# Clustered attention, a Fourier step and a feed-forward net in one Trainium2 kernel: rows 129 to 256 of the transform folded some ticks ahead of the sequence's end, sign images of two weight pieces at a time, and power-of-two scales worked out by way of PSUM

## The chip, the core and the metric

The kernel runs on one core of a Trainium2 chip. A core has five engines that run in parallel, each through its own list of instructions in order: PE (TensorE, matrix products), DVE (VectorE), ACT (ScalarE), POOL (GpSimd) and SP (which here only issues DMA transfers). Engines wait for one another through semaphores. Data lie in SBUF (128 partitions) and in PSUM, into which PE writes its products and which DVE and ACT read and write as well. The metric is the device time of one execution in microseconds (us).

## The reference

Inputs are q, k and v (4 sequences x 8 heads x 768 rows x 64), 16 centroids of 64 numbers for each head, and two weight matrices (512 x 2048 and 2048 x 512), all float32.

```
q_n, k_n, c_n = q/|q|, k/|k|, centroids/|centroids|
mask   = argmax_c(q_n . c_n)[:, None] == argmax_c(k_n . c_n)[None, :]
attn   = softmax(where(mask, q @ k.T / 8, -1e9))      # rows over 768 keys
x      = concat over heads of attn @ v                # 4 x 768 x 512
mixed  = real(fft(fft(x, axis=1), axis=2))            # over 768 rows, then 512 columns
u      = x + mixed
un     = (u - mean(u)) / sqrt(var(u) + 1e-6)          # per row
out    = u + relu(un @ w_ch1) @ w_ch2
```

A row attends only to keys of its own cluster. The real part of the two transforms needs, of a transform over 512 columns, cosine and sine products; since cosine is even and sine odd, column 512-j can be added to (or subtracted from) column j first, which halves the product. The same holds over the 768 rows. The kernel calls both steps folding.

## The kernel before, in words

**Number format.** A float32 operand of a product is written as two float16 halves (high and low), and the product is made of three float16 products. Making the halves is called halving: ACT writes the high half, DVE the low one (`halve`, L641 and L642). Each tensor is first scaled by a power of two that is found from its largest magnitude: `top_power` (L55 to L61) takes the exponent's bits with a shift (L58), an addition with a maximum (L59) and a minimum with a multiplication (L60), and ends with a reciprocal (L61); the first three work in integers on a few numbers per partition.

**Attention.** Two heads of one sequence make a pair, 16 pairs in all (pair 0 to 15, four per sequence). Each pair has six steps of 128 rows; a step is called a tick here, and tick n is step (n - 5) mod 6 of pair (n - 5) // 6, so that pair 4, the first of the second sequence, begins at tick 29. In a tick, `scores` makes the products of 128 rows with all 768 keys for both heads into two PSUM tiles (L320), adds the mask by a product of cluster codes (L325, whose operand `oht` is the transposed "one-hot" code), then DVE scales them and finds the row's largest (L339), ACT takes the exponential (L343 for pairs 0 to 3, L345 later) and writes its high half (L353), POOL the low half (L354), and SP issues a transposing DMA of each half (L356). One tick later `attend` multiplies them with v (L374 to L376), and DVE divides by the row sums into the tile X (L386 to L390). X holds [128, 6, 512]: the 768 x 512 rows of one sequence; there are two X tiles, used in turn. For pairs 0 to 3 the second X tile serves as the exponential's buffer; from pair 4 on, L339 writes its output to a bf16 tile `ju` that nobody reads (only the row's largest is used), and L345 reads PSUM.

**One-hot codes.** For the next pair, products with the centroids stand in a PSUM slot; DVE subtracts the largest into the tile `ac` (L277, L279), POOL adds a term for ties (L281), DVE finds the largest again (L285) and writes the codes (L289, L293), POOL two small parts of them (L298, L300), and SP transposes them into `oht` (L303). `ac` has one buffer.

**Weights.** In ticks 0 to 28 the weights are loaded in 32 pieces of 128 x 512 and changed to halves: a DMA into one of eight raw buffers, the largest magnitude (L491), then for the first matrix one scale per row block (L496 or L504, then `top_power`, 128x1 or 128x4), two ACT instructions that take two sign images of the top 16 bits (`signs`, L519 and L520, 128x512 each, into one of two buffers `PN`), a product that joins them to the piece (PE L528, DVE L532), and halving (L538, L541, L542, L544). A PSUM pool `psf` of three 128x512 slots serves this, the scales, the Fourier step and the feed-forward net.

**Fourier and feed-forward.** Sequence b's attention ends two ticks after its last step, at tick 31, 55, 79 and 103. There `fold` runs: it subtracts X's row blocks 3 to 5 from blocks 0 to 2 (L660, 128x1536), folds the columns (L661, 128x765, on DVE for the subtraction and on POOL for the sum), halves 256 columns (L641, L642, 128x768) and transposes both halves in one DMA (L667); then the same for the sum. Both use one buffer `XF`. The transform's products (L713, L728), the row transform, the norm, `up` (L858) and `down` (L888) of sequence b are spread over the ticks of sequence b + 1's attention; after tick 103 there is no attention left and they run alone.

**Order.** PE's order is written by hand: a planner gives each call a tick and a place in the tick (for instance `at(t, 0, self.fft.fold, b)`), and fills the ticks with the Fourier and feed-forward products up to a due time. The other engines' orders are decided by a scheduler from the same calls, so that code placed elsewhere moves instructions of other work as well.

## Time and profile before

| what | value |
|---|---|
| runs shown, us | 1053.73, 1049.66, 1053.15 (median 1053.15) |
| profiled execution: own time, us | 1049.91 |
| its span (first to last instruction), us | 1048.1 |
| PE busy | 910.8 us, 87% |
| DVE busy | 627.4 us, 60% |
| ACT busy | 625.3 us, 60% |
| POOL busy | 586.9 us, 56% |
| mean share of the 16 DMA engines, 45 to 205 us | 0.96 |

Times in rows are microseconds from the start of the span, unless marked ns. A group's row reads: line, engine, operation, output <- inputs with shapes, count | busy time, mean ns of one | idle time of that engine just before them and what ended it. A row of waits reads: engine, what it was about to do <- engine and instruction (or transfer) that it waited for: total us, times, longest. A row of the timeline reads: start, duration, engine, instruction, and in brackets the idle time before it. A row of windows gives a stretch's length, then busy us (and count) of PE, PE's weight loads, DVE, ACT and POOL, the granted PE clock, and the share of DMA. Ticks are not marked in the profile; they are counted from the groups of L320. In this execution tick 25 begins at 177.4, 29 at 206.1, 31 at 219.6, 33 at 246.4, 50 at 393.0, 74 at 614.1; the last sequence's fold (tick 103) begins at 882.5. Attention's last tick begins at 854.9.

### The profile page before, as it was taken

Reading aid. Unit: us, or ns where it says so; the run is one execution under the profiler, and the core shown is the slowest. Engines: PE = TensorE matmul, PEld = TensorE weight load, DVE = VectorE, ACT = ScalarE, POOL = GpSimd, SP = SyncE. Lnnn points to the kernel's source line nnn. Section 1 sums busy time; section 2 is a strip of 40 time slices with the busy share of each in tenths; the row PEclk is TensorE's granted clock in tenths of the full one; section 3 lists DMA queues with packets and bytes.
Section 4 is the critical chain, followed back from the end, with each engine's and each line's share of the span. In section 5 each row is a group of like instructions: output and inputs, shape, how many; then the busy total and the mean of one; then the engine's idle time right before and its main releaser. Section 6 shows DMA issues by size and latency. Waiting matters only on the chain.

```text
span 1048.1 us, 23542 instructions
## 1 busy us (share of the span) xinstructions
PE 910.8 (87%) x9350; PEld 591.7 (56%) x9362; DVE 627.4 (60%) x1297; ACT 625.3 (60%) x980; POOL 586.9 (56%) x693
## 2 busy tenths in 40 slices
PE   3665565749899999998899999997999999999998
PEld 2333333425575756655666757555757667576674
DVE  8789899767757555668656555667555333631110
ACT  4798889755766665645666746556756543351230
POOL 2364565753975756655856646647847645271230
PEclk9987878769899999999899999998999999999999
DMA  7799998979887776568877767588757562321000
GB/s 272 179 225 245 196 239 166 171 156 153 177 123 153 128 154 121 121 137 161 153 137 142 140 128 132 110 141 170 124 102 133 96 110 43 81 52 31 11 11 21
DMA packets 396239, 140.01 MB, mean 134 GB/s; under 512 B 381784, under 2 KB 381792, under 8 KB 396128
## 3 DMA queue, kind: packets, MB, share of 16 engines
q1 hardware_dynamic: 396128, 138.50, 65.9%
q8 instruction: 73, 1.20, 0.5%
q14 instruction: 38, 0.31, 0.1%
HBM read 42.52 MB, written 6.29 MB: 47 GB/s over the span
## 4 chain that ended last, share of the span: by engine, by line
PE 39%; DVE 6%; DMA 3%; ACT 3%; POOL 2%; issue 2%; SPq 0%; ACTq 0%; DVEq 0%; POOLq 0%
PE ps_f L888 16%; PE ps_f L858 13%; PE ps_big L320 3%; DMA pt<-ph 3%; PE ps_f L713 2%; DVE ju L339 1%; ACT p L345 1%; PE ps_o L374 1%; POOL ph L354 1%; PE ps_o L375 1%; PE ps_o L376 1%; PE ps_big L325 1%; ACT ph L353 1%; DMA scr<-in_k_dram 0%; DVE arena L660 0%
## 5 line engine op out<-in xcount | busy, mean ns | idle before, releaser
L354 POOL TENSOR_TENSOR ph<-p,ph 128x768 f16<-128x768 f32 x144 | 242.9, 1688 | 184.6 <-ACT ph L353 150.1
L858 PE MATMUL ps_f<-arena,w1h 128*128 128x256 f16 x1536 | 271.4, 277 | 19.1 <-ACT arena L866 9.0
L888 PE MATMUL ps_f<-w2h,arena 128*128 128x512 f16 x768 | 238.9, 379 | 0.0
L345 ACT ACTIVATE p<-ps_big,rmx,sce 128x768 f32<-128x768 f32 x144 | 142.1, 988 | 132.9 <-DVE ju L339 127.5
L858 PE MATMUL ps_f<-arena,w1l 128*128 128x256 f16 x768 | 212.4, 277 | 0.0
L339 DVE TENSOR_SCALAR_CACHE_REDUCE ju<-ps_big,sce 128x768 bf16<-128x768 f32 x144 | 146.1, 1014 | 68.2 <-PE ps_big L325 58.2
L888 PEld LDWEIGHTS <-arena 128*128 128x128 f16 x1152 | 108.7, 98 | 126.6 <-issue 5.2
L858 PEld LDWEIGHTS <-w1h 128*128 128x128 f16 x1536 | 152.1, 99 | 36.0 <-issue 14.3
L867 POOL TENSOR_TENSOR arena<-arena 128x256 f16<-128x256 f32 x192 | 128.1, 677 | 77.3 <-ACT arena L866 73.6
L320 PE MATMUL ps_big<-hlk,hlq 64*128 64x384 f16 x1152 | 128.9, 348 | 39.0 <-ACT p L345 23.4
L374 PE MATMUL ps_o<-v,pt 128*128 128x66 f16 x1152 | 124.8, 198 | 43.0 <-DVE X L390 27.5
L888 PE MATMUL ps_f<-w2l,arena 128*128 128x512 f16 x384 | 145.5, 379 | 0.0
L374 PEld LDWEIGHTS <-pt 128*128 128x128 f16 x1152 | 110.2, 100 | 57.7 <-issue 37.1
L353 ACT CAST ph<-p 128x768 f16<-128x768 f32 x144 | 119.6, 832 | 15.0 <-DMA pt<-ph 12.8
L375 PE MATMUL ps_o<-v,pt 128*128 128x64 f16 x1152 | 124.8, 199 | 0.0
L376 PE MATMUL ps_o<-v,pt 128*128 128x66 f16 x1152 | 124.5, 198 | 0.0
L866 ACT ACTIVATE arena<-ps_f,wrel 128x256 f16<-128x256 f32 x192 | 90.1, 472 | 54.8 <-DVE arena L863 54.7
L863 DVE TENSOR_SCALAR arena<-ps_f,wrel 128x256 f32<-128x256 f32 x96 | 46.3, 482 | 124.9 <-PE ps_f L858 66.4
L320 PEld LDWEIGHTS <-hlq 64*128 64x128 f16 x1152 | 55.5, 99 | 101.5 <-issue 72.7
L375 PEld LDWEIGHTS <-pt 128*128 128x128 f16 x1152 | 110.7, 101 | 2.8
L376 PEld LDWEIGHTS <-pt 128*128 128x128 f16 x1152 | 111.1, 103 | 0.0
L858 PEld LDWEIGHTS <-w1l 128*128 128x128 f16 x768 | 76.1, 99 | 20.2 <-issue 10.7
(178 smaller groups left out, 1330.4 us busy)
## 6 DMA issues: line engine op xcount, KB each, us to landing
arena<-in_moe_w_ch_dram SPq DMA_DIRECT2D x32, 512.0 KB, 6.8
scr<-in_q_dram SPq DMA_DIRECT2D x16, 384.0 KB, 2.9
scr<-in_k_dram SPq DMA_DIRECT2D x16, 384.0 KB, 4.5
vst<-in_v_dram SPq DMA_DIRECT2D x16, 384.0 KB, 3.5
out_dram<-arena SPq DMA_DIRECT2D x24, 256.0 KB, 2.3
pt<-ph SPq DMA_TRANSPOSE x168, 3.9
arena<-in_cs_dram SPq DMA_DIRECT2D x12, 192.0 KB, 3.5
arena<-in_ss_dram SPq DMA_DIRECT2D x12, 192.0 KB, 3.5
```

Of the source, the lines that this page charges most:

```text
L320: nc.tensor.matmul(out=ps[j][:, hf, 0:SH], lhsT=hq[rows[j], a, sl], rhs=hk[rows[j], c, hs], start=(i == 0), stop=False)
L339: self.mark = nc.vector.tensor_scalar(out=ju, in0=ps[j][:, :, 0:SH], scalar1=ne, scalar2=None, op0=ALU.mult, op1=ALU.min, accum_out=m)
L345: nc.scalar.activation(x, ps[j][:, :, 0:SH], AF.Exp, bias=m, scale=e)
L353: nc.scalar.copy(out=ph[:, 0], in_=p32)
L354: nc.gpsimd.tensor_tensor(out=ph[:, 1], in0=p32, in1=ph[:, 0], op=ALU.subtract)
L374: nc.tensor.matmul(out=o[:, at:at + W], lhsT=hi, rhs=v16[:, kt, 0:W], start=(kt == 0), stop=False)
L375: nc.tensor.matmul(out=o[:, at:at + D], lhsT=hi, rhs=v16[:, kt, 66:130], start=False, stop=False)
L376: nc.tensor.matmul(out=o[:, at:at + W], lhsT=lo, rhs=v16[:, kt, 0:W], start=False, stop=(kt == ST - 1))
L858: nc.tensor.matmul(out=ps.rearrange("p (t x) -> p t x", x=P), lhsT=a[:, dc, fs], rhs=c[:, :, dc], start=(i == 0), stop=(i == 11))
L866: nc.scalar.activation(hh[:, f], ps, AF.Relu, scale=rel[:, f:f + 1])
L867: nc.gpsimd.tensor_tensor(out=hl[:, f], in0=r, in1=hh[:, f], op=ALU.subtract)
L888: nc.tensor.matmul(out=ps, lhsT=a[:, f, ts], rhs=c[:, f], start=(i == 0), stop=(i == 47))
```

## The change

Four things are changed.

**Scales by way of PSUM.** `top_power` gets a second operand `t` for its intermediate results. For 128x1 it is the PSUM column into which the largest is now reduced; for 128x4 it is four columns of a fresh `psf` slot (four times in the run). L58, L59 and L60 then read or write PSUM; only L60's result and the reciprocal stay in SBUF.

**Signs of two pieces.** `signs` runs for every second piece and takes two pieces in one instruction, 128x1024, into buffers `PN2`.

**L339 in place.** For pairs 4 to 15, L339 writes its scaled scores over the scores in PSUM, in float32, and the exponential reads them with scale -1; `ju` is gone, and the arena of SBUF that the weights and the Fourier step share grows by 3072 B per partition.

**The fold in two halves.** Column j is folded with column 512-j, so columns 128 to 255 need X's column blocks 1 and 2 only (128 columns each, written by a sequence's second and third pair), and columns 0 to 127 blocks 0 and 3. `early` folds, halves and transposes the first kind, the difference six ticks and the sum four ticks ahead of the sequence's end (ticks t-6 and t-4 for t = 31, 55, 79, 103), in a tile taken from `ac`, pinned behind the tick's last L339. `fold` at tick t does the rest: DVE adds 128x768, then 128x381, ACT and DVE halve 128x384 instead of 128x768, and each transposing DMA moves 6 blocks instead of 12 (four DMAs of 6 per sequence for two of 12). All folding is on DVE now; POOL's L661 goes, five small POOL copies come. The two folds of `fold` have a buffer each. The columns 0, 128 and 256 that stand at the seams change places, and the constants with them (`dft_constants`, `c128`, `first`); `even` and `odd` take columns 128 to 255 first.

Knobs that come with it (`KEEP0`, `WAIT`, `N1`) have the values that leave the order of the calls as it was. PE's list is the same as before but for the operands' names. The lists of the others change: DVE has 36 rows more, ACT 24 fewer, POOL 16 more, SP 8 more.

```diff
-def top_power(nc, tops, s, inv):
-    t = tops.bitcast(I32)
-    nc.vector.tensor_scalar(out=t, in0=t, scalar1=20, scalar2=None, op0=ALU.logical_shift_right)
+def top_power(nc, tops, t, s, inv):
+    t = t.bitcast(I32)
+    nc.vector.tensor_scalar(out=t, in0=tops.bitcast(I32), scalar1=20, scalar2=None, op0=ALU.logical_shift_right)
     nc.vector.tensor_scalar(out=t, in0=t, scalar1=-910.0, scalar2=1.0, op0=ALU.add, op1=ALU.max)
...
-            ju = x if early else sb.tile([P, 2, SH], BF16, name="ju", tag="ju")
+            ju = x if early else ps[j][:, :, 0:SH]
             self.mark = nc.vector.tensor_scalar(out=ju, in0=ps[j][:, :, 0:SH], scalar1=ne, ..., accum_out=m)
-                nc.scalar.activation(x, ps[j][:, :, 0:SH], AF.Exp, bias=m, scale=e)
+            nc.scalar.activation(x, ju, AF.Exp, bias=m, scale=-1.0)
...
     def scales(self, g, mx):
         s = self.sb.tile([P, 4], F32, name="wsc", tag="wsc", bufs=2)
-        top_power(self.nc, mx, s[:, 0:n], ...)
+        t = self.psf()[:, 0:n] if n > 1 else mx
+        top_power(self.nc, mx, t, s[:, 0:n], ...)
...
     def signs(self, k):
+        if self.JOINT:
+            if k % 2 == 0:
+                pn = at(self.PN2[k // 2 % 2], [P, 2, 2, DM], BF16)
+                raw = at(self.RAW[k % len(self.RAW)], [P, 2, 4 * DM + 16], U16)
+                top = raw[:, :, 4:4 + 4 * DM].rearrange("p a (n f) -> p a n f", f=4)[:, :, :, 0]
+                nc.scalar.activation(pn[:, 0].bitcast(I16), top.bitcast(I16), AF.Relu, ...)
+                nc.scalar.activation(pn[:, 1].bitcast(I16), top, AF.Relu, ...)
+            return
...
+    def prepared(self, b, buf, blocks, i, op):
+        nc.vector.tensor_tensor(out=buf.rearrange("p (z t x) -> p t z x", z=2, t=3), in0=x[0], in1=x[1], op=op)
+        f = buf.rearrange("p (z t x) -> p z t x", z=2, t=3)
+        first, second = f[:, 0, :, 0:1], f[:, 1, :, 0:1]
+        if blocks[0]:
+            nc.gpsimd.tensor_copy(out=self.c128[:, i], in_=first)
+            if i == 0:
+                nc.gpsimd.tensor_copy(out=first, in_=second)
+        else:
+            if i == 0:
+                nc.gpsimd.tensor_copy(out=self.first, in_=first)
+            nc.vector.tensor_tensor(out=first, in0=self.c128[:, i], in1=second, op=op)
+        nc.vector.tensor_tensor(out=f[:, 0, :, 1:P], in0=f[:, 0, :, 1:P], in1=f[:, 1, :, P - 1:0:-1], op=op)
+        h = buf[:, SH:2 * SH].bitcast(F16).rearrange("p (a t x) -> p a t x", a=2, t=3)
+        self.halve(f[:, 0], h[:, 0], h[:, 1], self.scale[b][0])
+        t = self.arena.at(self.XT[i][blocks[0]], [P, 6, P], F16)
+        nc.sync.dma_start(out=t, in_=h.rearrange("p a t x -> p (a t x)"), transpose=True)
+
+    def early(self, b, k):
+        i, op = self.FOLDS[k]
+        buf = self.pool.tile([P, 2, ST * 4, NC_], F32, name="ac", tag="ac").rearrange("p a g c -> p (a g c)")
+        self.parts[b][i, 1] = self.prepared(b, buf, (1, 2), i, op)
+
     def fold(self, b):
         for i, op in self.FOLDS:
-            f = at(self.XF, [P, 3, DM], F32)
-            self.engine(self.FE[i]).tensor_tensor(out=f, in0=X[:, 0:3], in1=X[:, 3:6], op=op)
-            self.engine(self.FE[2 + i]).tensor_tensor(out=f[:, :, 1:M], in0=f[:, :, 1:M], in1=f[:, :, DM - 1:M:-1], op=op)
-            h = at(self.XH, [P, 2, 3, M], F16)
-            self.halve(f[:, :, 0:M], h[:, 0], h[:, 1], s)
-            nc.sync.dma_start(out=t, in_=h.rearrange("p a t x -> p (a t x)"), transpose=True)
+            buf = at(self.XF + 3072 * i, [P, 2 * SH], F32)
+            self.parts[b][i, 0] = self.prepared(b, buf, (0, 3), i, op)
...
+    E, KEEP0 = (-6, -4), 21.0
...
             at(t, -1, self.drain, self.KEEP0)
+            for k in range(2):
+                at(t + self.E[k], 4.6, pin, self.fft.early, b, k)
             at(t, 0, self.fft.fold, b)
```

Three places in DVE's list of instructions show how the change moves work. Rows read: line of that version, operation, output<-inputs, shape, and x2 for two in a row. L491, L532, L544, L660, L642, L390, L388 and L386 of before are L489, L540, L552, L666, L655, L387, L385 and L383 of the change.

DVE in the weights' stage, at the second of the four 128x4 scales and the finish of attention's rows beside it (116 us in the profile; X_63 is the first X tile, X_64 the second, winv_86 the table of inverse scales). Before:

```order
L386 TENSOR_SCALAR rs<-ps_o,scp 128x6
L289 TENSOR_TENSOR oh<-ac,mx 128x12x16
L293 TENSOR_TENSOR oh<-ac,mx 128x6x16 x2
L532 SCALAR_TENSOR_TENSOR ps_f<-arena,ps_f 128x512 x2
L388 RECIPROCAL rs<-rs 128x6
L339 TENSOR_SCALAR X_64,rmx<-ps_big,sce 128x768 x2
L390 TENSOR_TENSOR X_63<-ps_o,rs 128x3x128
L491 TENSOR_REDUCE arena<-arena 128x1
L544 SCALAR_TENSOR_TENSOR w2l<-ps_f,wsc,w2h 128x512
L58 TENSOR_SCALAR arena<-arena 128x4
L59 TENSOR_SCALAR arena<-arena 128x4
L60 TENSOR_SCALAR winv_86<-arena 128x4
```

And of the change:

```order
L383 TENSOR_SCALAR rs<-ps_o,scp 128x6
L540 SCALAR_TENSOR_TENSOR ps_f<-arena,ps_f 128x512
L285 TENSOR_REDUCE mx<-ac 128x24
L59 TENSOR_SCALAR ps_f<-ps_f 128x4
L540 SCALAR_TENSOR_TENSOR ps_f<-arena,ps_f 128x512
L385 RECIPROCAL rs<-rs 128x6
L289 TENSOR_TENSOR oh<-ac,mx 128x12x16
L293 TENSOR_TENSOR oh<-ac,mx 128x6x16 x2
L60 TENSOR_SCALAR winv_86<-ps_f 128x4
L387 TENSOR_TENSOR X_63<-ps_o,rs 128x3x128
L339 TENSOR_SCALAR X_64,rmx<-ps_big,sce 128x768 x2
L61 RECIPROCAL wsc<-winv_86 128x4
```

The three scale instructions are the same, but their intermediate results stand in a `psf` slot (ps_f), and they stand some rows earlier, among the finish of the tick's attention.

DVE in ticks 26 to 28, where pair 4's codes are made. Before:

```order
L339 TENSOR_SCALAR X_64,rmx<-ps_big,sce 128x768 x2
L277 TENSOR_REDUCE mx<-ps_f 128x24
L279 TENSOR_TENSOR ac<-ps_f,mx 128x384
L285 TENSOR_REDUCE mx<-ac 128x24
L339 TENSOR_SCALAR X_64,rmx<-ps_big,sce 128x768 x2
L289 TENSOR_TENSOR oh<-ac,mx 128x12x16
L293 TENSOR_TENSOR oh<-ac,mx 128x6x16 x2
L386 TENSOR_SCALAR rs<-ps_o,scp 128x6
```

And of the change, starting at the row behind the L277 that answers to the second one above:

```order
L678 TENSOR_TENSOR ac<-ac 128x3x127
L339 TENSOR_SCALAR X_64,rmx<-ps_big,sce 128x768 x2
L655 SCALAR_TENSOR_TENSOR ac<-ac,vseq 128x384
L383 TENSOR_SCALAR rs<-ps_o,scp 128x6
L590 TENSOR_REDUCE arena<-ps_f 128x1
L385 RECIPROCAL rs<-rs 128x6
L591 RECIPROCAL arena<-arena 128x1
L593 TENSOR_SCALAR dsc<-arena 128x1
L387 TENSOR_TENSOR X_63<-ps_o,rs 128x3x128
L592 TENSOR_SCALAR wrel<-wrel,arena 128x16
L339 TENSOR_SCALAR X_64,rmx<-ps_big,sce 128x768
L279 TENSOR_TENSOR ac<-ps_f,mx 128x384
```

The early fold (L666 on X_63, ahead of L277, then L678 and L655) has `ac`; L279, which writes `ac` for pair 4, has moved behind the finish of the tick's attention (L383 to L387) and the first L339 of tick 28; L285, L289 and L293 stand behind the second L339 of that tick.

DVE at the first sequence's end, tick 31. Before:

```order
L390 TENSOR_TENSOR X_63<-ps_o,rs 128x3x128
L660 TENSOR_TENSOR arena<-X_63 128x1536
L248 TENSOR_REDUCE amx<-vst 128x1
L642 SCALAR_TENSOR_TENSOR arena<-arena,vseq 128x768
L339 TENSOR_SCALAR ju,rmx<-ps_big,sce 128x768
L660 TENSOR_TENSOR arena<-X_63 128x1536
L339 TENSOR_SCALAR ju,rmx<-ps_big,sce 128x768
L201 SCALAR_TENSOR_TENSOR v_2839<-vst,scp,v_2839 128x6x64
L661 TENSOR_TENSOR arena<-arena 128x3x255
L642 SCALAR_TENSOR_TENSOR arena<-arena,vseq 128x768
```

And of the change:

```order
L387 TENSOR_TENSOR X_63<-ps_o,rs 128x3x128
L666 TENSOR_TENSOR arena<-X_63 128x3x2x128 x2
L248 TENSOR_REDUCE amx<-vst 128x1
L677 TENSOR_TENSOR arena<-c_88,arena 128x3
L678 TENSOR_TENSOR arena<-arena 128x3x127 x2
L655 SCALAR_TENSOR_TENSOR arena<-arena,vseq 128x384
L339 TENSOR_SCALAR ps_big,rmx<-ps_big,sce 128x2x384 x2
L201 SCALAR_TENSOR_TENSOR v_2826<-vst,scp,v_2826 128x6x64
L677 TENSOR_TENSOR arena<-c_88,arena 128x3
L655 SCALAR_TENSOR_TENSOR arena<-arena,vseq 128x384
```

Both folds of the tick, of half the width, and one of the two low halves stand ahead of its two L339 (before: one whole fold and its low half ahead of the first L339, the other fold between the two); the other low half stands behind both.

98 lines of the change are left out of this document (54 added, 44 removed).

## The prediction

> **What bounds the kernel now.** I read the windows first, cut where the kind of work changes: start, weights beside the first sequence's attention, that sequence's end, the long middle, and the part behind attention.
>
> ```profile
> core 0: us, PE busy (x) PEld busy (x) DVE busy (x) ACT busy (x) POOL busy (x), PEclk, DMA share, GB/s
> 0.00:45.00 45.00, 22.02 (x103) 9.57 (x105) 35.11 (x93) 27.68 (x42) 10.63 (x43) 1.00 0.72 229
> 45.00:205.00 160.00, 98.50 (x1249) 60.98 (x1259) 139.54 (x282) 138.64 (x198) 97.97 (x84) 0.82 0.96 208
> 205.00:275.00 70.00, 48.98 (x536) 29.46 (x536) 50.65 (x102) 39.72 (x57) 40.74 (x39) 0.79 0.87 158
> 275.00:860.00 585.00, 559.90 (x6157) 370.14 (x6156) 355.24 (x725) 361.64 (x561) 371.41 (x426) 0.98 0.72 134
> 860.00:1048.00 188.00, 181.37 (x1317) 121.60 (x1313) 46.85 (x96) 57.58 (x124) 66.13 (x103) 1.00 0.16 37
> ```
>
> From 275 us on, PE is busy for 741.3 of 773 us: what other engines save there is worth nothing unless it ends a PE wait. In 45 to 205 us PE is busy for 98.5 of 160, while DVE (139.5) and ACT (138.6) have 87% each and DMA 0.96. So I read that stage's waits, to see who comes last.
>
> ```profile
> PE ps_o L374 <- DVE X L390: 27.5, 6, 5.5
> ACT X L343 <- DVE X L339: 7.6, 5, 2.5
> ACT w2h L538 <- DVE ps_f L532: 5.8, 6, 2.7
> ACT w1h L538 <- DVE wsc L61: 3.4, 2, 3.0
> DVE arena L491 <- DMA arena<-in_moe_w_ch_dram: 6.5, 6, 2.0
> DVE amx L248 <- DMA vst<-in_v_dram: 3.5, 2, 3.1
> ```
>
> PE waits for DVE's finish, and ACT waits 16.8 us for DVE, most of its 21.4 us idle. DVE itself idles 20.5 us, 10 of them for weights and v that haven't landed. So DVE is the last engine of this stage, with DMA close behind: microseconds off DVE count until transfers stop them.
>
> **Scales.** The groups of DVE in 45 to 205 us, by form:
>
> ```profile
> L60 DVE TENSOR_SCALAR winv<-arena 128x4 int32<-128x4 int32 x4 | 6.2, 1547 | 0.1
> L59 DVE TENSOR_SCALAR arena<-arena 128x4 int32<-128x4 int32 x4 | 4.6, 1143 | 0.1
> L58 DVE TENSOR_SCALAR arena<-arena 128x4 int32<-128x4 int32 x4 | 0.8, 211 | 0.0
> L60 DVE TENSOR_SCALAR winv<-arena 128x1 int32<-128x1 int32 x3 | 0.5, 150 | 0.0
> L410 DVE TENSOR_SCALAR scp<-ps_f 128x3 f32<-128x3 f32 x3 | 0.5, 162 | 0.1
> L491 DVE TENSOR_REDUCE arena<-arena 128x1 f32<-128x512 bf16 x22 | 15.0, 681 | 6.7 <-DMA arena<-in_moe_w_ch_dram 6.5
> ```
>
> Four numbers take L60 1547 ns, one number 150, so the time isn't arithmetic; three numbers read from PSUM (L410) take 162. With an operand in PSUM I price each of the three at 162: 4 x (211 + 1143 + 1547) = 11.6 us become 4 x 3 x 162 = 1.9, which takes 9.7 us off the last engine. The 128x1 cases stay as they are (150 against 162). Bounds: 9.7 if DVE alone sets the stage, 0 if the landings do; nothing in L410's row makes it a loss. I take 7, since DVE is the last waited for in 27.5 + 16.8 us of waits and the landings in 10.
>
> [...]
>
> Two costs come with it. A fresh `psf` slot is held four times while L58 to L60 stand among other work (the first place of the order), on a pool of three that PE's joins (L528) need: nothing at best, four holds of 1 us (two L339's rows) at worst; I take 0.5. One more L491 now stands ahead of the first scales: 0.7 by its row.
>
> **Signs.** ACT's groups of the same stage:
>
> ```profile
> L519 ACT ACTIVATE arena<-arena 128x512 int16<-128x512 int16 x26 | 19.6, 755 | 2.2 <-PE ps_o L376 1.5 <-PE ps_f L528 0.7
> L199 ACT ACTIVATE v<-vst,scp 128x384 f16<-128x384 f32 x6 | 3.6, 617 | 0.0
> L343 ACT ACTIVATE X<-X,rmx 128x768 f32<-128x768 f32 x44 | 40.4, 936 | 9.3 <-DVE X L339 7.6 <-POOL ph L354 1.4 <-issue 0.3
> ```
>
> From 384 to 768 columns ACT pays (936 - 617) / 384 = 0.83 ns a column, so 1024 columns cost 755 + 512 x 0.83 = 1180 where two instructions cost 1510. That is 0.33 us, twice for each of the stage's 13 pairs: 8.6 us off ACT. But ACT's idle time already ends in DVE's instructions, and the second sign image now comes up to one piece early, the first up to one late. Bounds 0 and 8.6; I take 1.
>
> **L339 in place.** DVE writes PSUM in L532 (688 ns for 512 columns, in the same view), in proportion no dearer than L339's SBUF write:
>
> ```profile
> L339 DVE TENSOR_SCALAR_CACHE_REDUCE X<-ps_big,sce 128x768 f32<-128x768 f32 x44 | 43.0, 1010 | 1.8 <-PE ps_big L325 1.3 <-POOL ac L281 0.5
> L532 DVE SCALAR_TENSOR_TENSOR ps_f<-arena,ps_f 128x512 uint32<-128x512 uint32 x28 | 18.9, 688 | 3.3 <-PE ps_f L528 3.2
> ```
>
> I take 0. If it were 0.1 us more for each of 144, 14 us of DVE would lie under PE's 741 busy us, and only the six ticks ahead of 275 us would feel 1 us.
>
> **The first sequence's end.** PE is busy for 49.0 of 70 us here. The timeline of DVE and POOL at tick 31:
>
> ```profile
> 220.65 1.76 DVE L660 TENSOR_TENSOR arena<-X 128x1536 f32<-128x1536 f32 x1
> 227.35 1.41 DVE L642 SCALAR_TENSOR_TENSOR arena<-arena,vseq 128x768 f16<-128x768 f32 x1 [3.23 <-ACT arena L641]
> 228.69 1.00 DVE L339 TENSOR_SCALAR_CACHE_REDUCE ju<-ps_big,sce 128x768 bf16<-128x768 f32 x1
> 220.88 3.02 POOL L354 TENSOR_TENSOR ph<-p,ph 128x768 f16<-128x768 f32 x1 [0.94 <-POOL v L200]
> 224.54 1.80 POOL L661 TENSOR_TENSOR arena<-arena 128x765 f32<-128x765 f32 x1
> ```
>
> L339 stands behind L642, which waits 3.2 us for a fold that lies behind POOL's L354. With all folding on DVE and half the width (the third place of the order), two folds of 0.9, two of about 0.5 and L642 of 0.7 precede L339, with a wait for ACT's half: it starts near 226.6, and the second L339 follows at once and not behind a second fold (1.75). I take a gain of 3; the most is 3.2 + 1.8 (a second L660) + 1.5 (half of L660 and L642) = 6.5, the least 0, if what is late next, POOL's L354, keeps the pace.
>
> **The tile `ac`.** Pair 4's codes pay for the early fold (the second place of the order).
>
> ```profile
> 198.54 1.04 DVE L289 TENSOR_TENSOR oh<-ac,mx 128x192 bf16<-128x192 f32 x1
> 201.18 1.60 SPq L303 DMA_TRANSPOSE oht<-oh  x1
> 208.52 1.02 DVE L339 TENSOR_SCALAR_CACHE_REDUCE ju<-ps_big,sce 128x768 bf16<-128x768 f32 x1 [0.70 <-PE ps_big L325]
> 214.92 1.46 PE L320 MATMUL ps_big<-hlk,hlq 64*128 64x384 f16 x8 [3.92 <-ACT p L345]
> pt<-ph SPq DMA_TRANSPOSE x168, 3.9
> ```
>
> L279 must now wait until the early half is transposed out of `ac` (3.9 us for a transpose of that size), and L289 and L293 stand a tick later, behind both its L339. A tick takes 7.2 here (25 to 29 from 177.4 to 206.1). With some 1 us of that wait on top, the codes leave 8 us later than 201.2, near 209.5, land near 213.5, and the first L339 of pair 4, at 208.5 now, waits for them: 5 to 6 us with the mask's product ahead of it. Beside it PE has a wait of 3.92 for ACT's L345 at 211 to 215, which takes part of that in. I take a loss of 3, between 0 and 6.
>
> Pairs 8 and 12 (ticks 50 and 74) come while PE is busy. Tick 50, DVE, ACT and PE:
>
> ```profile
> 398.17 0.56 DVE L279 TENSOR_TENSOR ac<-ps_f,mx 128x384 f32<-128x384 f32 x1
> 402.55 1.02 DVE L339 TENSOR_SCALAR_CACHE_REDUCE ju<-ps_big,sce 128x768 bf16<-128x768 f32 x1
> 405.43 0.99 ACT L345 ACTIVATE p<-ps_big,rmx,sce 128x768 f32<-128x768 f32 x1
> 408.84 1.15 PE L320 MATMUL ps_big<-hlk,hlq 64*128 64x384 f16 x12
> ```
>
> Queued behind a waiting L279 are L285 to L293 and the L339 at 402.55. The second exponential of that tick frees its PSUM tile at 406.4, and PE needs it at 408.8: a spare of 2.4 us. A wait of 2 us, about half of a landing, stays below it, though the transposes behind the exponential come later too. Loss 1 for both together, between 0 and 8 (two full landings).
>
> The other folds, and the last one, lie under PE's busy 741 us: 0. If that cover were gone, 3 us apiece.
>
> **Sum.** 7 + 1 - 0.7 - 0.5 + 3 - 3 - 1 = 5.8 off the profiled execution's 1049.9 (span 1048.1, 1.8 around it), 1044.1. That execution lies 3.2 below the runs' median; the mean of it and the three runs is 1051.6, so I forecast **1046**.
>
> **Rivals.** (1) *Landings hold the stage.* DMA share is 0.96 already; if weights and v keep their dates, the 9.7 us only lengthen DVE's 10 us of waits, the stage gives 1 to 2 us and the whole 1051 (+3, -3 and -1 as above). Against it: a part of the stage has run at a higher share.
>
> ```profile
> 45.00:75.00 30.00, 18.92 (x233) 11.77 (x235) 24.58 (x59) 26.23 (x38) 20.86 (x16) 0.89 1.03 222
> ```
>
> At 1.03 the 160 us could be 149.
>
> (2) *Full relief.* ACT's 8.6 us end waits too, since L343 stands behind the sign images in ACT's order: 9.7 + 4 in the stage, 11.5 with the rest as above, and 1040. For it: ACT is as busy as DVE. Against: the waits name DVE.
>
> (3) *One `ac` buffer; slower.* Here SP's transposes wait for POOL's halves, and the early half's transpose is queued behind them. If it lands a whole landing (4 us) later than I assumed, L279 blocks DVE for 6 us ahead of L339 in ticks 51 and 75, 3.6 beyond the spare of 2.4, so 7 for both in place of 1, and pair 4's own bound of 6 and the first-sequence gain of 3 are gone too, 6 more. That is 12 us worse than the sum: 1058. It decides from a block of 2.4 us on. For it: a rank of SP transposes stands in every tick. Against: PE's other waits may cover some.
>
> (4) *Collisions with POOL.* Some DVE instructions with two SBUF inputs come out far longer than the same form does at other times. One line's view and the other of its kind:
>
> ```profile
> L660 DVE TENSOR_TENSOR arena<-X x8: 1748/1758/3085, 220.6 to 888.2; 128x1536 f32<-128x1536 f32 x8
> L661 DVE TENSOR_TENSOR arena<-arena x4: 944/1616/2277, 233.7 to 890.0; 128x765 f32<-128x765 f32 x4
> ```
>
> The change has 14 of these per sequence for 5, so if half were 1.3 us longer, the first sequence would lose 9 x 0.5 x 1.3 = 6 on DVE; 4 of it in the time, two thirds as PE has the other third of that stretch to spare (49.0 busy of 70), give 1050.
>
> [...]
>
> **How the numbers follow.** Chances: forecast 0.36, (1) 0.18, (2) 0.20, (3) 0.18, (4) 0.08. About 0.5%, 5.3 us, is what a measurement can tell from no change. Faster: 0.25 of the forecast, 0.02 of (1), all of (2): 0.47. Slower: 0.02, 0.01, 0, 0.15 and 0.02: 0.20. The rest, 0.33, is the same. The forecast's own range by the bounds is 1042 to 1050. The 8-in-10 range takes in (1), (2) and (4) and reaches to the middle of (3): 1037 to 1058.
>
> **What would show it.** Right: the 128x4 rows of L59 and L60 near 0.16 us; attention's tick 25 some 7 us earlier than 177.4; 32 sign rows near 1.18 us; L339 at tick 31 free of the 3.2 us wait; a PE wait for pair 4's codes of 2 to 6 us. Wrong: DVE's DMA waits in the stage grown by what the scales gave up (1), ACT's waits gone along with DVE's (2), L279 waiting for SP's transpose for 4 us and PE idle at ticks 51 and 75 (3), or the new fold rows with a mean well over 1 ns a column (4).

## The result, and the profile after

The change makes the kernel slower: 1079.83 us (median of four runs, 1076.65 to 1080.04) where the kernel before takes 1053.44 (four runs, 1049.66 to 1055.48). The ratio is 1.0253, with a 95% interval of 1.0227 to 1.0278. Forecast was 1046, with a range of 1037 to 1058.

The windows of the changed kernel, cut at the same times as those of before (the last one is 30 us longer):

```profile
45.00:205.00 160.00, 93.16 (x1171) 56.03 (x1186) 128.27 (x267) 129.70 (x168) 92.68 (x79) 0.82 0.93 202
205.00:275.00 70.00, 49.31 (x511) 30.36 (x512) 51.44 (x96) 32.07 (x48) 31.74 (x31) 0.71 0.79 144
275.00:860.00 585.00, 544.56 (x5941) 360.13 (x5942) 366.42 (x750) 349.11 (x566) 374.02 (x439) 0.97 0.70 132
860.00:1078.00 218.00, 210.84 (x1629) 138.49 (x1623) 61.84 (x129) 69.48 (x141) 80.00 (x120) 1.00 0.24 47
```

DVE and ACT are both less busy in the weights' stage, and less of the work gets done in it. Where the time went is seen best from the ticks. PE's list is the same in both kernels, so the start of each tick's first L320 can be compared (us; the difference of the two timelines):

```
tick         11    22    28    29    30    33    40    52    53    57    76    77    100
before     73.6 157.1 198.0 206.1 210.7 246.4 310.8 408.8 417.3 462.1 631.2 641.1 854.9
changed    80.5 165.0 207.2 215.3 225.2 261.6 328.5 429.0 441.3 487.5 658.0 669.8 884.2
later by    6.9   7.9   9.2   9.2  14.5  15.2  17.7  20.2  24.0  25.4  26.8  28.7  29.3
```

So there are three losses: 9 us beside the weights, 8.5 from pair 4's beginning to the end of pair 5 (5.3 of them from tick 29 to 30), and 11.6 in the long middle (3.8 of them at tick 53, pair 8's first, 1.9 at tick 77, pair 12's first).

**Beside the weights.** The groups of DVE in 45 to 205 us, by form:

```profile
L59 DVE TENSOR_SCALAR ps_f<-ps_f 128x4 int32<-128x4 int32 x4 | 0.6, 162 | 0.0
L58 DVE TENSOR_SCALAR ps_f<-arena 128x4 int32<-128x4 int32 x4 | 0.6, 160 | 0.0
L60 DVE TENSOR_SCALAR winv<-ps_f 128x4 int32<-128x4 int32 x4 | 0.6, 156 | 0.0
L489 DVE TENSOR_REDUCE arena<-arena 128x1 f32<-128x512 bf16 x22 | 15.0, 683 | 18.3 <-DMA arena<-in_moe_w_ch_dram 18.1
```

The twelve 128x4 scale instructions cost 1.9 us for 11.6, as worked out. But L489 (L491 of before) now waits 18.1 us for weights where it waited 6.5.

**Pair 4.** Rows of the timeline about its codes, of DVE, SP and PE:

```profile
210.59 0.55 DVE L279 TENSOR_TENSOR ac<-ps_f,mx 128x384 f32<-128x384 f32 x1
214.43 0.60 DVE L293 TENSOR_TENSOR oh<-ac,mx 128x96 bf16<-128x96 f32 x2
218.80 1.58 SPq L303 DMA_TRANSPOSE oht<-oh  x1
222.54 0.51 PE L325 MATMUL ps_big<-oht 32*128 32x384 bf16 x4 [5.81 <-DMA oht<-oh]
223.09 1.03 DVE L339 TENSOR_SCALAR_CACHE_REDUCE ps_big<-ps_big,sce 128x768 f32<-128x768 f32 x1 [1.12 <-PE ps_big L325]
```

The codes leave at 218.80, 11.6 us behind the start of tick 28 (201.18 and 3.2 us before), and PE waits 5.81 for them.

**Tick 31.** The two folds of what is left at the sequence's end (the eight of the run take 0.95 to 5.14 us, with a median of 0.96):

```profile
233.45 6.01 DVE L666 TENSOR_TENSOR arena<-X 128x768 f32<-128x768 f32 x2
233.50 1.49 POOL L703 TENSOR_TENSOR arena<-arena,X 1x255 f32<-1x255 f32 x1 [0.78 <-DVE X L387]
234.95 1.63 POOL L351 TENSOR_TENSOR ph<-p,ph 128x768 f16<-128x768 f32 x1
237.01 1.63 POOL L351 TENSOR_TENSOR ph<-p,ph 128x768 f16<-128x768 f32 x1
```

DVE needs 6.0 us for them, beside instructions of POOL: the first fold takes 0.96, the second 5.13 (234.32 to 239.46), and it ends 0.8 us behind the second L351, at 238.64.

### The profile page after: what moved, and what is told of

It is laid out like the page before. It is cut to its first block, busy times and chain, and to the rows that moved or that the text cites. A ratio compares the mean times of both kernels' runs of the same rounds, so it can differ in the third digit from the quotient of the medians.

```text
span 1078.3 us, 23547 instructions
## 1 busy us (share of the span) xinstructions
PE 919.1 (85%) x9342; PEld 594.3 (55%) x9362; DVE 643.5 (60%) x1333; ACT 607.9 (56%) x956; POOL 588.5 (55%) x709
## 4 chain that ended last, share of the span: by engine, by line
PE 39%; DVE 17%; DMA 15%; POOL 11%; ACT 11%; issue 8%; SPq 0%; POOLq 0%; ACTq 0%; DVEq 0%
PE ps_f L927 16%; PE ps_f L897 12%; DMA pt<-ph 7%; POOL ph L351 5%; PE ps_big L320 3%; ACT ph L350 3%; DMA arena<-in_moe_w_ch_dram 3%; DVE ps_big L339 3%; DVE X L339 2%; ACT p L342 2%; PE ps_f L752 2%; DMA vst<-in_v_dram 2%; POOL arena L906 1%; DMA pt<-p 1%; PE ps_o L371 1%
## 5 line engine op out<-in xcount | busy, mean ns | idle before, releaser
L351 POOL TENSOR_TENSOR ph<-p,ph 128x768 f16<-128x768 f32 x144 | 241.3, 1683 | 181.6 <-ACT ph L350 157.2
L897 PE MATMUL ps_f<-arena,w1h 128*128 128x256 f16 x1536 | 272.5, 277 | 22.9 <-ACT arena L905 15.3
L342 ACT ACTIVATE p<-ps_big,rmx 128x768 f32<-128x768 f32 x144 | 128.6, 900 | 126.3 <-DVE ps_big L339 111.5
L320 PE MATMUL ps_big<-hlk,hlq 64*128 64x384 f16 x1152 | 135.9, 362 | 42.3 <-ACT p L342 22.6
L906 POOL TENSOR_TENSOR arena<-arena 128x256 f16<-128x256 f32 x192 | 130.5, 691 | 72.6 <-ACT arena L905 68.3
L339 DVE TENSOR_SCALAR_CACHE_REDUCE ps_big<-ps_big,sce 128x768 f32<-128x768 f32 x144 | 141.5, 1020 | 43.4 <-PE ps_big L325 40.0
L905 ACT ACTIVATE arena<-ps_f,wrel 128x256 f16<-128x256 f32 x192 | 90.5, 474 | 69.1 <-DVE arena L902 67.4
L902 DVE TENSOR_SCALAR arena<-ps_f,wrel 128x256 f32<-128x256 f32 x96 | 46.1, 480 | 124.2 <-POOL arena L906 76.4
L320 PEld LDWEIGHTS <-hlq 64*128 64x128 f16 x1152 | 57.4, 101 | 105.8 <-issue 77.1
```

Source lines behind the costliest of these rows:

```text
L320: nc.tensor.matmul(out=ps[j][:, hf, 0:SH], lhsT=hq[rows[j], a, sl], rhs=hk[rows[j], c, hs], start=(i == 0), stop=False)
L339: self.mark = nc.vector.tensor_scalar(out=ju, in0=ps[j][:, :, 0:SH], scalar1=ne, scalar2=None, op0=ALU.mult, op1=ALU.min, accum_out=m)
L342: nc.scalar.activation(x, ju, AF.Exp, bias=m, scale=-1.0)
L351: nc.gpsimd.tensor_tensor(out=ph[:, 1], in0=p32, in1=ph[:, 0], op=ALU.subtract)
L897: nc.tensor.matmul(out=ps.rearrange("p (t x) -> p t x", x=P), lhsT=a[:, dc, fs], rhs=c[:, :, dc], start=(i == 0), stop=(i == 11))
L905: nc.scalar.activation(hh[:, f], ps, AF.Relu, scale=rel[:, f:f + 1])
```

## The experiments

Theories, with the names that the expectations use. *Queue*: the scheduler has put three of the weights' largest-magnitude instructions (L491) a tick earlier into DVE's list than their piece lands, and DVE stands still in front of them. *Landing*: transfers set the stage, whatever DVE does. *Signs*: the signs of two pieces cost the stage. *One buffer*: `ac` holds up the codes. *Collision*: DVE's instructions with two SBUF inputs wait for POOL's. *POOL*: the fold's small copies stand behind POOL's long instructions.

### One part at a time

The kernel before with one part of the change, or the changed kernel without one.

The scales alone:

> The kernel before with only the scales by way of PSUM. In its DVE list three of the weights' largest-magnitude instructions (L491 of before, the 14th, 16th and 17th) stand a tick earlier than before, ahead of the landing of their piece, as in the changed kernel. Queue theory (those instructions hold DVE's list while the piece lands): 5 to 12 us slower than before, about 1061, with DVE's waits for weights near 18 us in the weights' stage instead of 6.5. Signs theory (the stage is lost to the signs of two pieces, the scales are a gain): 4 to 9 us faster than before, about 1046.

Signs alone:

> The kernel before with only the sign images of two pieces at a time. As predicted (8.6 us off ACT, which ends in DVE's waits anyway): 1 us faster, 1050 to 1054 where the kernel before is 1053. Rival (a pair of pieces has to be there before either is joined, and ACT is held 2.4 us at a stretch ahead of attention's exponentials): 4 to 8 us slower.

Scores alone:

> The kernel before with only the last part of the scores changed: L339 writes over the scores in PSUM, the exponential reads them with an immediate scale. As predicted: no change, 1051 to 1055. Rival by the changed kernel's rows (the read of the row maximum 140 ns in place of 83, the exponential 900 in place of 988, 144 times each): DVE 8 us more, ACT 13 us less, between 3 us faster and 3 us slower.

All but the early fold, and the early fold with the scores' part:

> The changed kernel with the Fourier step of the kernel before (one fold, at the sequence's end, POOL's part included). If the early fold costs what stands behind pair 4 (17 us of the 26.4): 1061 to 1065, and no PE wait for pair 4's codes. If the scales, signs and the scores' part lose the middle too: 1070 and more.

> The changed kernel with the scales and the sign images of the kernel before, so the early fold with the scores' part alone (without the latter the early fold doesn't fit into SBUF). If parts add up: 1080 less what the scales cost by themselves (11), so 1066 to 1071, with no loss up to tick 24. If the fold's loss hangs on the weights' stage being late: 1060 and less.

| kernel | median us | ratio to before, 95% |
|---|---|---|
| scales alone | 1063.37 | 1.0111 (1.0070 to 1.0152) |
| signs alone | 1053.81 | 1.0014 (0.9998 to 1.0030) |
| scores' part alone | 1055.53 | 1.0035 (1.0016 to 1.0054) |
| scales, signs, scores' part | 1062.88 | 1.0099 (1.0083 to 1.0115) |
| early fold and scores' part | 1072.57 | 1.0191 (1.0161 to 1.0221) |
| whole change | 1079.83 | 1.0253 (1.0227 to 1.0278) |

The scales, which were to be the gain, cost 1.1% by themselves. The early fold costs 1.5 to 1.6%: 1.0253 less 1.0099 beside the other three, 1.0191 less 1.0035 beside the scores' part alone. The signs do nothing that can be measured. The scores' part costs 0.35%; the parts by themselves add up to more than they do together (1.11 + 0.14 + 0.35 for 0.99), so part of that seems to overlap with the scales' loss; which part was not looked for.

### The scales: where L491 stands

One edit holds the largest-magnitude instructions of pieces 9 to 32 behind a given count of L339: that of before ("hold"), or two more, one tick later ("later hold").

```diff
-        nc.vector.tensor_reduce(out=mx[:, i:i + 1], in_=self.top(k).bitcast(BF16), op=ALU.max, ...)
+        n = self.HELD.get(k)
+        with self.tc.issue_after(self.att.marks[n - 1].ins) if n else contextlib.nullcontext():
+            nc.vector.tensor_reduce(out=mx[:, i:i + 1], in_=self.top(k).bitcast(BF16), op=ALU.max, ...)
```

> The same, with the largest-magnitude instructions of pieces 9 to 32 held behind the same count of L339 that they stood behind in the kernel before. Queue theory: the scales' 9.7 us off DVE show now, 3 to 8 us faster than before, about 1047, and 8 to 18 us faster than the run without the hold. Signs theory: as the run without the hold, within 2 us.

> The scales alone, with the largest-magnitude instructions held one tick later than in the kernel before. Queue theory (only DVE's place matters): DVE's waits for weights fall below 5 us and the time to 1046 to 1052. Landing theory (transfers hold the stage, whatever DVE does): no better than the hold at before's places, 1054 to 1060.

> The kernel before, nothing but the largest-magnitude instructions held one tick later: the control for the run of the scales with that hold (1050). If that run's 3 us are the hold's: 1049 to 1051. If they are the scales': 1053 and more.

> The changed kernel with the same hold on the largest-magnitude instructions. Queue theory: the weights' stage gets back 9 to 15 us, 1065 to 1071 in place of 1080. Signs theory: 1080 within 3 us, since the sign images are as they were.

| kernel | median us | ratio to before, 95% |
|---|---|---|
| scales, no hold | 1063.37 | 1.0111 (1.0070 to 1.0152) |
| scales, hold | 1055.97 | 1.0040 (1.0017 to 1.0062) |
| scales, later hold | 1050.10 | 0.9971 (0.9951 to 0.9992) |
| before, later hold | 1049.05 | 0.9977 (0.9958 to 0.9995) |
| whole change, hold | 1075.72 | 1.0230 (1.0192 to 1.0267) |

DVE's group of L491 in 45 to 205 us, in the kernel with the scales alone (L492 there) and with the later hold (L496):

```profile
L492 DVE TENSOR_REDUCE arena<-arena 128x1 f32<-128x512 bf16 x22 | 15.0, 683 | 13.6 <-DMA arena<-in_moe_w_ch_dram 13.4
```

```profile
L496 DVE TENSOR_REDUCE arena<-arena 128x1 f32<-128x512 bf16 x22 | 14.5, 685 | 0.0
```

The waits go from 13.4 us to nothing, and 13 us of the time with them. So the scales' loss is the place of L491 in DVE's list: the work is the same, a few instructions stand in front of a transfer that hasn't landed, and everything behind them on DVE stands too. The hold at before's places gave back less than expected in both kernels: 0.7% of the scales' 1.1%, and 0.2% of the whole change, which its intervals don't tell from nothing. With that hold DVE still waits for weights, from 0 to 205 us for 12.6 us with the scales alone and 16.1 in the whole change, where the kernel before has 7.9; that fits a DVE that comes earlier to the same place in its list than the piece lands. Why the scales with that hold are still 0.4% slower than the kernel before is not shown. And the control says the rest: the later hold is worth 2.4 us in the kernel before as well, so that of the scales' 9.7 us off DVE nothing is seen (0.9971 against 0.9977). A worth of 3 us could hide in these intervals, the 7 of the sum could not.

### What 9.7 us off DVE are worth with lighter transfers, and with ACT unloaded

Transfers made lighter, with the hold (the diff of the loads; part of the weights is left out):

```diff
+        w = 4 * DM if k < len(self.RAW) else 2 * DM
-        self.nc.sync.dma_start(out=raw[:, 1:1 + 4 * DM], in_=src.bitcast(U16))
+        self.nc.sync.dma_start(out=raw[:, 1:1 + w], in_=src.bitcast(U16)[:, 0:w])
```

> The kernel before with the largest-magnitude instructions held at their own places, and from the ninth weight piece on only the left half of the piece loaded (the right half keeps an earlier piece, so part of the weights is wrong). Landing theory: DVE's waits for weights vanish and the stage shortens by 4 to 10 us: 1043 to 1049. Queue theory: DVE's work sets the stage, 1050 to 1054.

> The same with the scales by way of PSUM (the same part of the weights left out). Landing theory: with the transfers out of the way the 9.7 us off DVE show, 5 to 9 us faster than the run with half pieces and the old scales. If the two runs agree within 2 us, DVE's busy time doesn't set the stage even without the transfers, and the first step of the prediction fails for that reason.

And scales and signs together, with the later hold:

> Scales by way of PSUM and signs of two pieces, with the hold one tick later. If DVE and ACT bound the weights' stage together (each 87% busy), taking 9.7 us off one and 8 us off the other shows now: 1040 to 1046. If the stage hangs on a chain through POOL's halves and SP's transposes, which neither part shortens: 1049 to 1052.

| kernel | median us | ratio to before, 95% |
|---|---|---|
| half pieces, hold | 1051.23 | 0.9985 (0.9965 to 1.0006) |
| half pieces, hold, scales | 1050.64 | 0.9984 (0.9964 to 1.0004) |
| scales, signs, later hold | 1052.32 | 1.0006 (0.9985 to 1.0027) |

The windows of the stage in the first two of these, and the first waits of the second:

```profile
45.00:205.00 160.00, 101.01 (x1262) 60.57 (x1259) 140.07 (x292) 141.12 (x202) 98.23 (x86) 0.81 0.89 175
45.00:205.00 160.00, 102.91 (x1280) 61.45 (x1278) 127.81 (x290) 141.60 (x204) 98.03 (x85) 0.81 0.88 175
```

```profile
POOL ph L355 <- ACT ph L354: 27.6, 12, 3.9
PEld L320 <- issue: 24.9, 44, 3.2
PEld L375 <- issue: 19.9, 14, 6.1
PE ps_o L375 <- DVE X L391: 16.4, 4, 5.7
ACT X L344 <- DVE X L339: 14.6, 9, 5.7
```

DVE is busy for 127.8 us of 160 where it was busy for 140.1, ACT waits longer for L339 than before (14.6 for 7.6), and the time is the same. With lighter transfers the scales give nothing, and with ACT unloaded (and whole pieces) they give nothing. So the busy time of DVE doesn't set the stage by itself, and neither does ACT's. The landings are not ruled out as firmly: half pieces take DMA's share from 0.96 to 0.89 and 0.88 only, and DVE still waits 4.1 and 7.0 us for weights; and no run lightens all three at once. The granted clock of the stage, 0.79 to 0.82 in these runs, doesn't explain it: scales and signs with the later hold have 0.82, as the kernel before, and gain nothing. The waits point to a chain from one tick to the next (L339, exponential, halves on ACT and POOL, SP's transpose, attend, finish), in which a wait for DVE is a wait for one instruction in its turn. That chain was not taken apart; what sets this stage stays open.

### The early fold: `ac`, and POOL

The early folds at ticks t-4 and t-2, so that none stands between a pair's cluster products and its codes in `ac`:

```diff
-    E, KEEP0 = (-6, -4), 21.0
+    E, KEEP0 = (-4, -2), 21.0
```

> The changed kernel with the two early folds at 4 and 2 ticks ahead of the sequence's end in place of 6 and 4, so that none stands between a pair's cluster products and its codes in the tile ac. One-buffer theory (a pair's codes wait for the early half's transpose): PE's wait for the codes at pair 4 (5.8 us) goes, and the losses at pairs 4, 8 and 12 (5, 5 and 3 us) with it: 1065 to 1070. Rival (the losses there come from the folding instructions themselves, their number or their collisions): 1080 within 3 us.

It took 1074.64 us, 1.0225 (1.0172 to 1.0277), and its trace starts tick 30 8.5 us behind before's and not 14.5, and tick 53 0.4 us later against tick 52 and not 3.8. PE has no wait for pair 4's codes. So the one buffer's loss at pairs 4 and 8 is gone. In the two traces this is worth 6 us at tick 100 (23.2 us behind before's start, and not 29.3); by the ratios it is 3 us, and their intervals overlap. The time lies between the two expectations, so something of the loss is not the buffer. What the early fold still costs in this kernel is 12 us against the change without it (1074.64 against 1062.88). Its ticks come later than those of that kernel by 5.3 us at tick 57, 5.8 at tick 77 and 12.2 at tick 79, so more than half of it falls at one sequence's end. DVE, POOL, ACT and PE at tick 79:

```profile
675.80 2.07 DVE L666 TENSOR_TENSOR arena<-X 128x768 f32<-128x768 f32 x1
678.65 2.59 DVE L678 TENSOR_TENSOR arena<-arena 128x381 f32<-128x381 f32 x1
681.16 1.10 DVE L677 TENSOR_TENSOR arena<-c,arena 128x3 f32<-128x3 f32 x1
```

```profile
675.41 1.64 POOL L351 TENSOR_TENSOR ph<-p,ph 128x768 f16<-128x768 f32 x1 [1.46 <-ACT ph L350]
679.16 1.63 POOL L351 TENSOR_TENSOR ph<-p,ph 128x768 f16<-128x768 f32 x1
```

```profile
682.30 0.61 ACT L654 ACTIVATE arena<-arena,vseq 128x384 f16<-128x384 f32 x1 [2.36 <-DVE arena L677]
683.99 0.47 ACT L905 ACTIVATE arena<-ps_f,wrel 128x256 f16<-128x256 f32 x1 [1.08 <-DVE arena L902]
```

```profile
684.52 0.27 PE L897 MATMUL ps_f<-arena,w1h 128*128 128x256 f16 x1 [2.76 <-ACT arena L905]
```

Three folding instructions take 5.8 us, one of them 1.10 for three columns. ACT's halving (L654) waits 2.36 for them. Behind the fold, in DVE's list and in ACT's, stand the evictions of the feed-forward net: L902 on DVE at 683.48, L905 on ACT, which waits for L902, and PE waits 2.76 for L905.

First the small copies of the fold, on ACT and not on POOL (`nc.gpsimd.tensor_copy(out=self.c128...)`, `first` and `self.first` become `nc.scalar.copy`):

> The changed kernel with the early folds at 4 and 2 ticks ahead and the folds' small copies (of columns 0, 128 and 256) on ACT in place of POOL. POOL theory (the fold's chain stands behind POOL's 1.65 us instructions, and ACT's halving with all that is queued behind it): 3 to 6 us faster than with the copies on POOL, 1069 to 1072. Collision theory (what is slow is DVE's instructions with two SBUF inputs, which stay): 1074 within 2 us.

1073.70 us, 1.0198 (1.0154 to 1.0243): no difference that can be told from 1.0225. The copies aren't it. Then the price by itself:

> Nothing of the kernel's work: only DVE instructions of seven forms, eight each, first with POOL idle and then beside a row of POOL's 128x768 subtractions (float32 less float16 to float16, the form of the low halves). Collision theory: two SBUF inputs (128x768 and 128x3 sums, the 128x384 low half) take 0.95, 0.16 and 0.6 us alone, and 1 to 1.7 us more beside POOL; the 128x4 integer instruction on SBUF 0.15 alone and over 1 beside POOL, on PSUM 0.16 in both; a sum with one PSUM input the same in both. Rival (the long rows come from somewhere else): every form within 10% of its own time beside POOL.

```
form                              alone, ns        beside POOL, ns
128x4 integers, SBUF              L1065   163      L1073   1418
128x4 integers, PSUM              L1066   163      L1074    157
128x1 integers, SBUF              L1067   149      L1075    144
128x768 sum, two SBUF inputs      L1068   947      L1076    944
128x3 sum, two SBUF inputs        L1069   161      L1077   1476
128x384 sum, one input in PSUM    L1070   557      L1078    558
128x384 low half, two SBUF inputs L1071   548      L1079   1604
```

Three of its rows, from the groups of DVE by form:

```profile
L1079 DVE SCALAR_TENSOR_TENSOR h<-x,h 128x384 f16<-128x384 f32 x8 | 12.8, 1604 | 0.0
L1077 DVE TENSOR_TENSOR y<-x 128x3 f32<-128x3 f32 x8 | 11.8, 1476 | 0.3
L1073 DVE TENSOR_SCALAR i<-i 128x4 int32<-128x4 int32 x8 | 11.3, 1418 | 0.0
```

and of POOL (ns, shortest, median and longest):

```profile
L1097 POOL TENSOR_TENSOR lo<-a,r x72: 1635/1635/2480, 22.5 to 152.1; 128x768 f16<-128x768 f32 x72
```

The 128x4 integers on SBUF and two of the three forms with two SBUF inputs take 1.06 to 1.32 us longer beside POOL; the 128x384 sum with an operand in PSUM, which runs while POOL does, doesn't (558 ns for 557). That this is a wait for the end of POOL's instruction fits a row of the kernel before: its 128x4 L59 on SBUF at 116.50 us takes 1.61, beside POOL's L354, which starts at 116.44 and takes 1.64. The micro run's order is fixed, and it decides the other rows: the 128x4 integers on PSUM, the 128x1 integers and the 128x768 sum follow just behind the 128x4 integers on SBUF (a median of 1598 ns), and POOL's own row (up to 2480 ns for 1635) fits a POOL that waits for the sum. So this run alone doesn't show that the two small ones don't wait. Rows of the big kernels do: in the kernel before, the 128x1 L59 at 56.44 us takes 0.15 while POOL's L354 runs from 56.21 to 57.86, and in the changed one the 128x4 L60 with an input in PSUM takes 0.16 at 129.30, while POOL's L351 runs from 129.19 to 130.84.

Then in the kernel. With both mends (E at -4 and -2, later hold) the change still stood 13.5 us above the kernel with scales, signs and the old fold (1052.32):

> The changed kernel with both mends: early folds at 4 and 2 ticks ahead, largest-magnitude instructions held one tick later. If what is left of the fold's loss is collisions of DVE's instructions with POOL (some 4 us per sequence, of which two or three show): the scales' 11 us go, the fold keeps 10 to 12: 1060 to 1066. If the two mends cover all: 1050 to 1054.

It took 1065.79 us, 1.0137 (1.0114 to 1.0160). And with POOL's subtractions replaced by a clear in ticks t-5 to t+1 (those low halves are left out):

```diff
+            if (5 + 6 * pr + st - 31) % 24 in (19, 20, 21, 22, 23, 0, 1):
+                nc.gpsimd.memset(ph[:, 1], 0)
+            else:
                 nc.gpsimd.tensor_tensor(out=ph[:, 1], in0=p32, in1=ph[:, 0], op=ALU.subtract)
```

> Scales by way of PSUM, signs of two pieces, later hold and the old fold, but in ticks t-5 to t+1 around each sequence's end POOL only clears the low halves and doesn't compute them (so those low halves are left out). Reference for the next run: 1048 to 1053, as the run with the low halves (1052.3) less what POOL's shorter work gives.

> The changed kernel with both mends and the same low halves left out. It stood 13.5 us above its reference with them. Collision theory (POOL's 1.65 us subtractions hold up the fold's DVE instructions): 4 to 8 us above now, and the fold's rows near their lone times. If the fold's number of instructions and ACT's wait for it are the price: still 11 us and more above.

| kernel | old fold | early fold | difference |
|---|---|---|---|
| POOL's subtractions there | 1052.32, 1.0006 (0.9985 to 1.0027) | 1065.79, 1.0137 (1.0114 to 1.0160) | 1.3% |
| cleared near the ends | 1046.41, 0.9938 (0.9910 to 0.9965) | 1047.57, 0.9958 (0.9941 to 0.9975) | 0.2% |

The early fold's loss (with that of the scores' part, which the right-hand kernels have too) is gone with POOL's subtractions: 1.2 us are left where 4 to 8 were expected. A gain like the one that the prediction hoped for at the first sequence's end shows here too, but doesn't last: the early fold's kernel is 0.8 us ahead of the other at tick 31, 6.2 at tick 33 and 0.5 at tick 46. Rows of the same instructions of the early fold's kernel, with them (ns, shortest, median and longest) and without:

```profile
L670 DVE TENSOR_TENSOR arena<-X x8: 946/958/5140, 220.5 to 895.4; 128x768 f32<-128x768 f32 x8
L682 DVE TENSOR_TENSOR ac<-ac x8: 530/580/1870, 199.9 to 876.1; 128x381 f32<-128x381 f32 x8
L682 DVE TENSOR_TENSOR arena<-arena x8: 542/550/2587, 227.4 to 896.4; 128x381 f32<-128x381 f32 x8
```

```profile
L673 DVE TENSOR_TENSOR arena<-X x8: 954/960/1480, 216.2 to 881.0; 128x768 f32<-128x768 f32 x8
L685 DVE TENSOR_TENSOR ac<-ac x8: 533/540/627, 193.8 to 861.2; 128x381 f32<-128x381 f32 x8
L685 DVE TENSOR_TENSOR arena<-arena x8: 539/547/682, 219.4 to 882.1; 128x381 f32<-128x381 f32 x8
```

In the micro run both engines have longer rows (DVE up to 1604 ns for 548, POOL up to 2480 for 1635), and DVE's list has moved in some places where POOL's work is shorter, so the two runs don't part DVE's wait for POOL from POOL's for DVE.

## Why the prediction was wrong, point by point

**Sum.** It had 7 + 1 - 0.7 - 0.5 + 3 - 3 - 1, and what was measured is a loss of 26. The gains of 7 and 3 did not come, and the losses of 0.7, 3 and 1 were sized too small; by parts it is some 11 us for the scales and 16 for the early fold.

**What bounds the stage.** "So DVE is the last engine of this stage" and "microseconds off DVE count until transfers stop them": this step failed, and with it the term 7 and rival (2). Attention's tick 25, which was to come some 7 us earlier than 177.4, came at 187.0. The duration was right (11.6 us to 1.9). The worth was read from waits that name DVE, but those name an instruction and not DVE's load: with the list kept apart by the hold, DVE 12 us less busy changes nothing (0.9984 against 0.9985). Rival (1) gave nearly the right worth. Its mechanism, landings, is seen with the hold at before's places (12.6 us of waits for 7.9, from 0 to 205 us); but with the later hold DVE's waits for weights are gone and the gain still doesn't come, and lighter transfers didn't bring it out. What sets the stage in DVE's place stays open.

**The place of L491.** The prediction priced "one more L491" at 0.7. The row's duration was the wrong price for a moved instruction. In DVE's list the 14th, 16th and 17th of them stand two L339 earlier, which the order of the two kernels told; DVE's waits for weights went from 6.5 to 18.1 us, and the scales alone cost 11. Both bounds (9.7 and 0) had left a loss out: "nothing in L410's row makes it a loss" looked at the instruction and not at what moves up behind it.

**Signs.** The duration came out as worked out (1217 ns for 1180), the worth is none: 1.0014, with 0.9998 to 1.0030.

```profile
L521 ACT ACTIVATE arena<-arena 128x1024 int16<-128x1024 int16 x12 | 14.6, 1217 | 2.3 <-PE ps_f L536 2.3
```

**L339 in place.** Taken as 0, and measured 3.7 us (1.0035, clear of its interval). L339 itself is as predicted; not foreseen was the read of the row's maximum behind it. The groups of DVE and ACT, now and (behind them) before:

```profile
L339 DVE TENSOR_SCALAR_CACHE_REDUCE ps_big<-ps_big,sce 128x768 f32<-128x768 f32 x144 | 141.5, 1020 | 43.4 <-PE ps_big L325 40.0 <-ACT arena L905 3.4
L339 DVE DVE_READ_ACCUMULATOR ps_big<-ps_big,sce 128x1 f32 x144 | 20.2, 140 | 0.0
L342 ACT ACTIVATE p<-ps_big,rmx 128x768 f32<-128x768 f32 x144 | 128.6, 900 | 126.3 <-DVE ps_big L339 111.5 <-POOL ph L351 5.4 <-POOL rpow L880 3.3
```

```profile
L339 DVE DVE_READ_ACCUMULATOR ju<-ps_big,sce 128x1 f32 x144 | 11.9, 83 | 0.0
L345 ACT ACTIVATE p<-ps_big,rmx,sce 128x768 f32<-128x768 f32 x144 | 142.1, 988 | 132.9 <-DVE ju L339 127.5 <-POOL ph L354 5.4
```

The read takes 140 ns for 83, the exponential 900 for 988. That the 57 ns make the 3.7 us was not tried.

**The first sequence's end.** The gain of 3 became a loss: "two folds of 0.9" took 6.0 us. That is rival (4), which had a chance of 0.08 and was priced at 4 us, for the first sequence only. With and without POOL's subtractions, the early fold's cost differs by 1.1% (1.3 less 0.2), some 12 us; with them, its kernel is 0.9 us behind at tick 31, 5.9 at 57, 4.1 at 77 and 10.7 at 79.

**The tile `ac`.** The mechanism and its time were right: codes 8 us later, PE's wait 5.81 where "5 to 6" was worked out. Wrong was that PE's other wait takes part of it in; ticks 29 to 30 show 5.3. For pairs 8 and 12 a loss of 1 for both was taken because of a spare of 2.4 us; ticks 53 and 77 show 3.8 and 1.9. That is between the forecast and rival (3), and with the early folds moved the 3.8 are 0.4.

**The cover.** "The other folds lie under PE's busy 741 us: 0" failed too. PE's list is fixed, and what it needs next comes through the lists of ACT and DVE, in which L905 and L902 stand behind the fold. PE's waits for that group, before (275 us to the end) and now (285 us to the end):

```profile
PE ps_f L858 <- ACT arena L866: 9.0, 10, 1.3
```

```profile
PE ps_f L897 <- ACT arena L905: 15.3, 16, 2.2
```

So PE's busy time here didn't cover work that stands ahead of its inputs in the lists that make them: 15.3 us of waits for L905, for 9.0 for L866 before.

## What to carry to other kernels

An engine that is named last in the waits of a stage is not shown to be the stage's bound; before a microsecond off it is counted, ask what instruction the waits are for, and try an undisturbed list. A small edit in a kernel whose lists a scheduler makes must be priced by the two lists: an instruction that moved up in front of a transfer cost here its wait for the landing, with everything behind it (with the scales alone 13.4 us of waits for 6.5, and 1.1% of the time). And a DVE instruction with two SBUF inputs next to a loaded POOL took 1476 ns for 161 with no more than three columns, and at tick 31 5.13 us for 0.96, beside several of POOL's in a row. So each instruction more was one more chance to wait; that few long ones would have been cheaper here was not tried.

The fastest kernel that computes the whole result came out of a control: the kernel before with L491 held one tick later, 1049.05 us, 0.9977 (0.9958 to 0.9995), and the same with the scales, 1050.10, 0.9971 (0.9951 to 0.9992).

## What the runs showed of the hardware

- A 128x3 sum of two SBUF inputs takes 161 ns alone and 1476 beside POOL's 128x768 subtractions, a 128x4 integer instruction on SBUF 163 and 1418. That fits the scales of before (L59 and L60, 1143 and 1547 ns on average, on SBUF) and of the change (162 and 156, in PSUM), where POOL's instructions run beside some of them (L60 at 129.30 us). In the kernel before, the L59 at 116.50 us takes 1.61, and POOL's L354, which started 0.06 us ahead of it, 1.64: there the one that came second ended with the first. The second fold of tick 31 took longer than that, 5.13 us: between its start at 234.32 and its end at 239.46 POOL ran four instructions from start to end, and why DVE's did not come in between them is not shown.
- The read of an accumulated maximum takes 140 ns behind an L339 that writes PSUM and 83 behind one that writes SBUF (144 of each). The element type is not the reason: behind the L339 of pairs 0 to 3, which write float32 to SBUF, it takes 83 as well (48 of them).
- The exponential from PSUM takes 900 ns with an immediate scale and 988 with a scale from a tile, over 768 columns (144 of each).
